# Scaled v of two attention units made together, in a retention and MLP kernel with a rewritten schedule

## The chip, the cores and the metric

The kernel runs on one core of a Trainium2 chip. Its metric is the device time of one execution in microseconds, the median of several runs. The core has five engines with queues of their own: TensorE (PE, with its weight loads shown apart as PEld), VectorE (DVE), ScalarE (ACT), GpSimd (POOL) and SyncE (SP). Here POOL does little but issue the loads from memory that convert float32 to bfloat16; SP issues the transposing copies and the stores.

## The reference

There are 8 batches, 8 heads, 576 positions and 64 numbers per head. First comes causal attention without a softmax, in which a score is multiplied by a power of a per-head number `gamma`; its output, laid out as 4608 tokens of 512 numbers, goes through two matrix products with an exact GELU between them.

```python
scores = (1.0 / np.sqrt(D_)) * np.matmul(q, k.transpose(0, 1, 3, 2))
gamma = 1.0 - 2.0 ** (-5.0 - np.arange(H))
Dmat = np.where(rel >= 0, gamma[:, None, None] ** rel[None], 0.0)   # rel = row - column
x = np.matmul(scores * Dmat, v)          # then as 4608 x 512 tokens
h = x @ w_in                             # 512 -> 2048
out = (0.5 * h * (1.0 + erf(h / sqrt(2)))) @ w_out   # 2048 -> 512
```

## The kernel before

**Attention units.** The attention is done in chunks of 128 positions, with a running state carried from chunk to chunk. A *unit* is one chunk of one batch, all 8 heads (the last chunk has 64 positions; there one unit, a *tail*, holds two batches). Units come in pairs, two batches `j = 0, 1` of the same chunk; there are 36 units, and four units make a block of 512 tokens. For a unit the kernel loads q, k and v (`load_unit`, line 506; the copies on POOL are lines 518 and 522), turns q and k (on PE for units 0 to 9, `turn`, by transposing copies on SP later), multiplies them (`scores`), masks the scores on DVE (`chunk_masked`, `masked`), and multiplies by v (`inner`). The decay by `gamma` is split into a factor on v's rows and one on the output. The first factor is `dv`, one number per row and head; v times `dv` is the tile `vh` (`scaled_v`, line 819), made either by one DVE operation of 128x512 (line 826) or by eight ACT operations of 128x64, one per head (line 829). The list `VH_ACT` says which units take ACT. `vh` is read by `inner` and by `state`, which adds k times v to the running state `u`; a product with the state (`cross`) completes a later chunk. Units 0 to 3, and other units of chunk 0, use v itself in `inner`.

**The MLP.** For each of nine blocks the 512 tokens x 2048 hidden numbers are made in pieces. The weights of the first layer come as eight loads `wi0` to `wi7` (line 528), those of the second as `wo0` to `wo7` (line 531). In blocks 2 to 8 the hidden numbers fall in four parts per block, and a part is done either plainly (four pieces of 4 products with 512 columns) or as a *unit* in Strassen's manner: seven products for eight, each of 4 products with 256 columns, with sums before and after on DVE and ACT. `LAYOUTS` says which: `'10'` is two units interleaved, `'2'` one, `'p3'` a plain part. In block 0 the pieces of the pairs listed in `WIDE` take all 512 tokens in one product; the others follow the units, 128 tokens at a time. The second layer of blocks 1 to 8 is always in Strassen's manner.

**What sets the order.** The program is unrolled in Python, and the order on every engine is written by a planner (`Plan`) when the program is built: every operation has an assumed duration, dependencies and a due time, and the planner takes the next one that can start. The constants at the head (lines 168 to 202) are its knobs: `SHIFT`, `GAP_A`, `GAP_B`, `BEFORE`, `HOLD`, `LOOK` place attention stretches between products, `EASE` holds back `vh`, `ORDER` is the order of the loads on POOL, `SECOND` and `PRODUCTS` that of the Strassen products. Where PE has nothing to do before 16 us of planned time, the planner puts in products on zeros (`warm`); they are instructions like others. Semaphores follow from the dependencies, so a real delay is a wait.

**Buffers.** Loads go into `N_LD = 4` slots, each for a pair's q, k and v. `N_VH = 5` buffers of one unit each hold `vh`, `N_RET = 3` (for either half) the masked scores. The pair `kept`, units 2 and 3, has tiles of its own, since its state is wanted late.

Of the kernel before, what the change touches and what calls it, by code (L numbers as in the profile page):

```python
# [107 lines left out]
def kernel(  # L108
# [9 lines left out]
    nc = tc.nc  # L118
# [42 lines left out]
    def slot_of(i):  # L161
# [24 lines left out]
    GAP_A = 0.0  # L186
    GAP_B = 1.3
    SHIFT = {4: -1.5, 5: -11.5, 6: 1.0, 7: 3.0, 8: 4.0, 9: -1.5, 10: 1.0, 11: 1.0, 12: 1.5, 13: -3.0, 14: -1.0, 15: -0.5, 16: -5.0, 17: -4.5, 18: -1.5, 19: 3.5, 20: 6.5}
# [12 lines left out]
    PRODUCTS = "3251647"  # L201
# [276 lines left out]
    touched = {}  # L478
# [201 lines left out]
    def state(bp, ci):  # L680
# [115 lines left out]
    def gone(nm):  # L796
# [8 lines left out]
        elif kind == "st_b":  # L805
            for i in pair_of[key]:
                vh_ring.give(T["pe"] + 0.3)
                read(i, "state")
# [10 lines left out]
    def scaled_v(i, engine, heads=(0, H)):  # L819
        ci = units[i][1]  # L820
        if "vh" not in st[i]:
            vh_ring.take()
            st[i]["vh"] = vh_pool.tile([128, H, D], BF16, tag="vh", name="vh")
        vh = st[i]["vh"]
        if engine == "dve":
            nc.vector.tensor_tensor(vh, loaded[i][1], dv[:, :, ci:ci + 1].to_broadcast([128, H, D]), op=ALU.mult)  # L826
        else:
            for h in range(*heads):
                nc.scalar.activation(vh[:, h], loaded[i][1][:, h], AF.Copy, scale=dv[:, h, ci:ci + 1])  # L829
        if heads[1] == H:  # L830
            read(i, "v")
# [48 lines left out]
    for i in range(N_U):  # L880
# [14 lines left out]
        if i not in fine and i not in tails:  # L895
# [6 lines left out]
            add(f"inner{i}", "pe", 0.23, [f"mask{m}.1" for m in duo] + [f"land v{i}" if i in raw else f"vh{i}"], lambda i=i: inner(i),  # L902
# [23 lines left out]
        else:  # L926
# [3 lines left out]
            add(f"in_a{n}", "pe", 0.125, [f"mask{n}.0"] + [f"vh{m}" for m in duo], lambda: None, due + 4, DRAIN, banks=2, mode="quad")  # L930
            add(f"in_b{n}", "pe", 0.4, [f"in_a{n}", f"u{bp},{ci},0"] + ([f"u{bp},{ci - 1},1"] if ci else []), lambda: None,
                due + 4, DRAIN, mode="quad")
    for i in v_order:
        due = need[group_of[i]] + 3.0 if i not in kept else need[group_of[pair_of[1, 1][0]]] - 2.0
        n = v_order.index(i)
        room = lambda i=i, due=due: max(0.0 if "vh" in st[i] else vh_ring.at(), due - EASE if group_of[i] > 3 else 0.0)
        before = ["dv", f"land v{i}"] + ([f"vh{v_order[n - 1]}"] if n else [])
        if i in VH_ACT:
            step_ = H // PARTS
            for p in range(PARTS):  # L940
                name = f"vh{i}" if p == PARTS - 1 else f"vh{i}.{p}"
                add(name, "act", 0.2625 * step_, [f"vh{i}.{p - 1}"] if p else before,
                    lambda i=i, p=p, step_=step_: scaled_v(i, "act", (p * step_, p * step_ + step_)), due + p / PARTS, at=None if p else room)
        else:
            add(f"vh{i}", "dve", 0.6, before, lambda i=i: scaled_v(i, "dve"), due if group_of[i] > 1 or i in kept else VH_DUE, at=room)
    order_of_states = [(bp, ci) for bp in range(B // 2) for ci in range(NCI - 1)]
    for bp, ci in order_of_states:
        pair = pair_of[bp, ci]
        deps = [f"vh{i}" for i in pair] + [f"land k{i}" for i in pair if i]
# [714 lines left out]
```

## Time and profile before

| what | value |
|---|---|
| median of 3 runs | 281.17 us (280.98 to 282.06) |
| profiled execution, its own time | 281.36 us |
| its span, first to last instruction | 279.5 us |
| PE, weight loads, DVE, ACT, POOL busy | 271.7, 215.7, 229.8, 176.2, 110.2 us |
| scaled v on ACT | 152 operations, 41.8 us |
| scaled v on DVE | 17 operations, 11.5 us |
| loads of q, k, v and weights on POOL | none after 200 us |

The span is cut at the first and last instruction; the profiled execution's own time has 1.86 us around it. Of a group of instructions the profile gives the count, the engine time that they cover together, and the mean length of one; on engines that overlap neighbours the mean is larger than the time per instruction. In the timeline an instruction's end is less certain than its start, for PE above all, so distances between starts are used here. Some PE records are missing, so that a count in the timeline can be one or two short.

### The profile page before, as it was taken

What the parts mean: (1) busy time and instruction counts of PE and PEld (TensorE: products, weight loads), DVE (VectorE), ACT (ScalarE), POOL (GpSimd) and SP (SyncE); (2) the same over time, 40 slices, a digit from 0 to 9 for tenths busy, and PEclk for the clock granted to TensorE, in tenths of its full rate; (3) what the DMA queues carried; (4) which work ended last, traced back from release to release, by engine and by line L of the source; (5) the groups of instructions that cost most, each with busy time, mean ns of one, the idle gap of its engine ahead of it and who ended that gap; (6) DMA issues with size and microseconds to landing.
All of it is one profiled execution on the core that took longest, in us unless ns stands there. A gap on an engine that the chain in (4) does not pass through costs nothing.

```text
span 279.5 us, 8688 instructions
## 1 busy us (share of the span) xinstructions
PE 271.7 (97%) x3607; PEld 215.7 (77%) x3623; DVE 229.8 (82%) x440; ACT 176.2 (63%) x434; POOL 110.2 (39%) x139
## 2 busy tenths in 40 slices
PE   7899999999999999999999999999999999999995
PEld 2584566578888688858886888778888888888784
DVE  5950757499999997899989999988799989958841
ACT  7586425567839974795189625982695379618741
POOL 8967869847546067710526448305000000000000
PEclk9999999999999999999999999999999999999999
DMA  9999999999999999999999999999700040013013
GB/s 154 165 187 172 191 169 178 136 231 144 131 131 138 214 114 142 145 198 166 130 220 115 118 139 243 145 112 94 196 2 2 6 150 4 2 38 115 0 40 113
DMA packets 152374, 35.55 MB, mean 127 GB/s; under 512 B 141072, under 2 KB 148240, under 8 KB 152336
## 3 DMA queue, kind: packets, MB, share of 16 engines
q0 software_dynamic: 115792, 17.97, 101.3%
q1 hardware_dynamic: 34912, 16.26, 34.3%
q10 hardware_dynamic: 1632, 0.79, 1.1%
q8 instruction: 28, 0.46, 0.7%
q14 instruction: 10, 0.08, 0.1%
HBM read 36.70 MB, written 9.44 MB: 165 GB/s over the span
## 4 chain that ended last, share of the span: by engine, by line
PE 78%; DMA 11%; POOL 7%; issue 1%; ACT 1%; DVE 0%; POOLq 0%; ACTq 0%
PE oT L231 37%; PE zT L231 11%; PE hT L231 8%; PE yT L231 7%; DMA qk_ld<-in_k_dram 5%; PE o_ps L231 4%; DMA qk_ld<-in_q_dram 3%; DMA w_in<-in_moe_w_in_dram 3%; POOL qk_ld L522 3%; PE sc L231 2%; PE u_ps L231 2%; POOL v_ld L522 2%; POOL qk_ld L518 1%; POOL w_in L528 1%; ACT g L1217 0%
## 5 line engine op out<-in xcount | busy, mean ns | idle before, releaser
L231 PEld LDWEIGHTS <-g 128*128 128x128 bf16 x576 | 55.0, 98 | 13.1 <-DVE g L1004 0.3
L231 PEld LDWEIGHTS <-w_in 128*128 128x128 bf16 x528 | 47.2, 98 | 15.8 <-issue 0.2
L231 PEld LDWEIGHTS <-wi_sum 128*128 128x128 bf16 x460 | 44.6, 98 | 7.8 <-issue 0.9
L231 PE MATMUL hT<-xT,w_in 128*128 128x256 bf16 (+2 forms) x334 | 49.7, 292 | 0.6
L1104 ACT ACTIVATE g<-hT 128x512 bf16<-128x512 f32 (+1 forms) x58 | 32.1, 555 | 23.4 <-PE hT L231 22.6
L231 PE MATMUL oT<-w_out,g 128*128 128x256 bf16 (+1 forms) x315 | 45.4, 293 | 0.3 <-issue 0.2
L829 ACT ACTIVATE vh<-v_ld,dv 128x64 bf16<-128x64 bf16 x152 | 41.8, 345 | 1.4 <-DVE qkT L573 1.3
L1248 ACT COPY o_sb<-oT 128x512 f32<-128x512 f32 (+1 forms) x27 | 14.5, 539 | 42.2 <-PE oT L231 35.2
L231 PEld LDWEIGHTS <-s 128*128 128x128 bf16 x384 | 37.1, 98 | 4.7
L522 POOL DMA_DIRECT2D qk_ld<-in_q_dram x31 | 27.7, 896 | 31.5 <-DMA qkT<-qk_ld 23.7
L522 POOL DMA_DIRECT2D v_ld<-in_v_dram x31 | 27.9, 903 | 14.6 <-issue 5.0
L231 PE MATMUL oT<-w_sum,s 128*128 128x256 bf16 x256 | 31.8, 273 | 0.0
L231 PE MATMUL oT<-w_sum,g 128*128 128x256 bf16 x256 | 31.3, 273 | 0.0
L522 POOL DMA_DIRECT2D qk_ld<-in_k_dram x31 | 28.0, 903 | 5.8 <-DMA v_ld<-in_v_dram 5.2
L1217 ACT ACTIVATE g<-zT 128x512 bf16<-128x512 f32 x46 | 26.2, 605 | 2.2 <-PE zT L231 1.5
L657 DVE TENSOR_TENSOR ret<-sc,msk 128x512 bf16<-128x512 f32 x36 | 23.1, 680 | 0.5 <-PE sc L231 0.5
L860 DVE TENSOR_TENSOR xT<-o_ps,dqT 128x512 bf16<-128x512 f32 x26 | 16.7, 680 | 0.6 <-PE o_ps L231 0.6
L826 DVE TENSOR_TENSOR vh<-v_ld,dv 128x512 bf16<-128x512 bf16 x17 | 11.5, 683 | 6.6 <-DMA v_ld<-in_v_dram 6.6
L573 DVE COPY qkT<-qk_ps 128x512 bf16<-128x512 bf16 x17 | 6.7, 420 | 12.3 <-PE qk_ps L235 12.3
L1196 DVE TENSOR_TENSOR q<-q,zT 128x512 f32<-128x512 f32 x23 | 14.9, 681 | 2.1 <-PE zT L231 1.9
L1254 DVE TENSOR_TENSOR o_sb<-o_sb,oT 128x512 f32<-128x512 f32 (+1 forms) x18 | 11.2, 622 | 6.4 <-PE oT L231 4.0
L1226 DVE TENSOR_TENSOR zT<-q,zT 128x512 f32<-128x512 f32 x23 | 15.6, 690 | 1.0 <-PE zT L231 0.6
(174 smaller groups left out, 461.2 us busy)
## 6 DMA issues: line engine op xcount, KB each, us to landing
out_dram<-o_sb SPq DMA_DIRECT2D x29, 256.0 KB, 3.4
qk_ld<-in_k_dram POOLq DMA_DIRECT2D x31, 128.0 KB, 8.0
qk_ld<-in_q_dram POOLq DMA_DIRECT2D x31, 128.0 KB, 8.0
v_ld<-in_v_dram POOLq DMA_DIRECT2D x31, 128.0 KB, 7.6
w_in<-in_moe_w_in_dram POOLq DMA_DIRECT2D x8, 256.0 KB, 8.0
w_out<-in_moe_w_out_dram POOLq DMA_DIRECT2D x8, 256.0 KB, 7.9
out_dram<-o_sb SPq DMA_DIRECT2D x9, 128.0 KB, 2.4
v_ld<-in_v_dram POOLq DMA_DIRECT2D x8, 64.0 KB, 6.3
```

What stands on the lines that cost most here:

```text
L231: return nc.tensor.matmul(*args, **more)
L522: nc.gpsimd.dma_start(dst, src[2 * bp + j, :, ci * C:ci * C + C, :].rearrange("h s d -> s h d"))
L657: nc.vector.tensor_tensor(r, t, by, op=ALU.mult)
L826: nc.vector.tensor_tensor(vh, loaded[i][1], dv[:, :, ci:ci + 1].to_broadcast([128, H, D]), op=ALU.mult)
L829: nc.scalar.activation(vh[:, h], loaded[i][1][:, h], AF.Copy, scale=dv[:, h, ci:ci + 1])
L860: nc.vector.tensor_tensor(dst, o, dqT[:, :, ci * C:ci * C + C], op=ALU.mult)
L1104: nc.scalar.activation(g_of(t, m0)[:, m0 % 2:m0 % 2 + n, m0 // 8, lo:hi], hT, AF.Gelu)
L1196: nc.vector.tensor_tensor(q_, q_, chain[key]["Z"][1], op=ALU.subtract)
L1217: nc.scalar.activation(target(key, what), chain[key][n][1], AF.Gelu)
L1226: nc.vector.tensor_tensor(to, chain[key]["q"], z, op=ALU.add)
L1248: nc.scalar.copy(target(key, what), chain[key][n][1])
L1254: nc.vector.tensor_tensor(to, to, chain[key][n][1], op=ALU.add)
```

## The change

**The scaled v.** `scaled_v` now makes both units of a pair at once. The tile `vh` has room for two units, and there are three such buffers where there were five single ones. On ACT one operation per head covers both units (128 x 2 x 64 in one instruction); on DVE it's still one operation of 128x512 per unit, one behind the other. It starts when the v of both units has landed. A buffer comes free when the state product of the pair has read it. For the kept pair, v of both units now lies in one tile, `v_kept`, that one operation can read. Tails stay as they were, one operation of 128x64 per head.

**The schedule, searched anew.** The knobs have other values: fewer mask buffers (`N_RET` 2 for 3), another list for ACT, seven wide pairs in block 0 instead of five, another order of loads (`pos` first, q, k and v of units 1 to 3 ahead of most weights), other places for the attention stretches, block 12's scores no longer apart, block 4 with one pair interleaved less, block 6 with three Strassen units and a plain part instead of four units, block 8 with its parts in another order, another order of first-layer products within a unit. All instruction orders differ from those before.

```diff
-    N_VH = 5
-    N_RET = 3
+    N_VH = 3
+    N_RET = 2
-    VH_ACT = [6, 8, 10, 11, 12, 13, 14, 15, 16, 17, 19, 21, 22, 24, 27, 28, 31, 34, 35, 37]
+    VH_ACT = [4, 8, 10, 11, 12, 13, 14, 15, 17, 18, 19, 20, 21, 22, 23, 26, 29, 31, 34, 36]
-    SLACK = 0.2
+    SLACK = 0.05
-    WIDE = [2, 6, 14, 10, 4]
+    WIDE = [0, 14, 2, 6, 12, 4, 10]
-    GAP_A = 0.0
-    GAP_B = 1.3
+    GAP_A = 6.3
+    GAP_B = 0
-    APART = [6, 7, 12]
-    BEFORE = 6.1
+    APART = [6, 7]
+    BEFORE = 5.2
-    LOOK = 16
-    HOLD = 5.6
-    LAYOUTS = {2: ['10', '2', 'p3'], 3: ['01', '2', 'p3'], 4: ['1', '02', 'p3'], 5: ['01', '2', 'p3'], 6: ['01', '23'], 7: ['01', '23'], 8: ['10', '3p2']}
-    LEAD = 8.9
-    SPREAD = 7.7
-    EASE = 6.8
-    ORDER = ("k2 wi4 q1 q2 k3 pos k1 wi0 q3 v1 v3 v2 wi3 wi6 wi1 wi7 v4 q4 wi5 k5 wi2 k4 q5 v5 wo0 wo4 wo1 wo5 q9 "
-             "k7 k6 wo6 q6 q8 v10 q7 wo2 v6 wo7 v9 wo3 k10 q10 v7 k8 k9 v8").split()
+    LOOK = 12
+    HOLD = 6
+    LAYOUTS = {2: ['10', '2', 'p3'], 3: ['01', '2', 'p3'], 4: ['01', '2', 'p3'], 5: ['01', '2', 'p3'], 6: ['01', '2', 'p3'], 7: ['01', '23'], 8: ['2', '30', 'p1']}
+    LEAD = 9.0
+    SPREAD = 7.8
+    EASE = 9
+    ORDER = ("pos q1 k1 q3 k3 v2 q2 k2 v1 wi0 v3 wi4 wi7 wi1 wi3 wi2 wi5 wi6 v4 wo4 k5 k4 q5 q4 wo0 v5 q8 wo1 wo5 "
+             "q9 v7 k7 v10 wo2 wo6 q6 wo7 wo3 q7 v6 k6 k10 q10 k8 k9 v9 v8").split()
-    PRODUCTS = "3251647"
+    PRODUCTS = "3251476"
...
-                loaded[i] = (const.tile([128, 2, H, D], BF16, name=f"qk_ld{i}"), const.tile([128, H, D], BF16, name=f"v_ld{i}"))
+                if i == slot_of(i):
+                    v_kept.append(const.tile([128, 2, H, D], BF16, name="v_kept"))
+                else:
+                    tiles_of(slot_of(i))
+                loaded[i] = (const.tile([128, 2, H, D], BF16, name=f"qk_ld{i}"), v_kept[0][:, i - slot_of(i)])
...
+        vh_ring.give(T["pe"] + 0.3)
         for i in pair_of[bp, ci]:
-            vh_ring.give(T["pe"] + 0.3)
             read(i, "state")
...
-    def scaled_v(i, engine, heads=(0, H)):
-        ci = units[i][1]
-        if "vh" not in st[i]:
+    def scaled_v(n, engine, heads=(0, H)):
+
+        ci, duo = units[n][1], pair_with(n)
+        if "vh" not in st[n]:
             vh_ring.take()
-            st[i]["vh"] = vh_pool.tile([128, H, D], BF16, tag="vh", name="vh")
-        vh = st[i]["vh"]
+            t = vh_pool.tile([128, 2, H, D], BF16, tag="vh", name="vh")
+            for i in duo:
+                st[i]["vh"] = t[:, i - n]
+            st[n]["vh both"] = t
+        t = st[n]["vh both"]
+        if n in kept:
+            v_ld = v_kept[0]
+        else:
+            v_ld = slots[n][1]
         if engine == "dve":
-            nc.vector.tensor_tensor(vh, loaded[i][1], dv[:, :, ci:ci + 1].to_broadcast([128, H, D]), op=ALU.mult)
+            for i in duo:
+                nc.vector.tensor_tensor(t[:, i - n], v_ld[:, i - n], dv[:, :, ci:ci + 1].to_broadcast([128, H, D]), op=ALU.mult)
         else:
             for h in range(*heads):
-                nc.scalar.activation(vh[:, h], loaded[i][1][:, h], AF.Copy, scale=dv[:, h, ci:ci + 1])
+                nc.scalar.activation(t[:, :len(duo), h], v_ld[:, :len(duo), h], AF.Copy, scale=dv[:, h, ci:ci + 1])
...
+    v_order = [n for n in v_order if n == slot_of(n)]
     for i in v_order:
-        n = v_order.index(i)
+        n, many = v_order.index(i), len(pair_with(i))
-        before = ["dv", f"land v{i}"] + ([f"vh{v_order[n - 1]}"] if n else [])
+        before = ["dv"] + [f"land v{m}" for m in pair_with(i)] + ([f"vh{v_order[n - 1]}"] if n else [])
         if i in VH_ACT:
-                add(name, "act", 0.2625 * step_, [f"vh{i}.{p - 1}"] if p else before,
+                add(name, "act", (0.2625 if many == 1 else 0.315) * step_, [f"vh{i}.{p - 1}"] if p else before,
         else:
-            add(f"vh{i}", "dve", 0.6, before, lambda i=i: scaled_v(i, "dve"), due if group_of[i] > 1 or i in kept else VH_DUE, at=room)
+            add(f"vh{i}", "dve", 0.6 * many, before, lambda i=i: scaled_v(i, "dve"), due if group_of[i] > 1 or i in kept else VH_DUE, at=room)
```

The dictionary `SHIFT` has other values too (left out above), and the places that named `vh` of each unit as a dependency now name the pair's.

More of the change, by code (lines that the diff above doesn't have):

```diff
@@ L901 @@
                     lambda i=i, e=e: chunk_masked(i, e), due + 2.0 + 0.01 * e, at=ret_ring.at if not e else None)
-            add(f"inner{i}", "pe", 0.23, [f"mask{m}.1" for m in duo] + [f"land v{i}" if i in raw else f"vh{i}"], lambda i=i: inner(i),
+            add(f"inner{i}", "pe", 0.23, [f"mask{m}.1" for m in duo] + [f"land v{i}" if i in raw else f"vh{slot_of(i)}"], lambda i=i: inner(i),
                 due + 4, DRAIN, banks=1, mode="col")
@@ L929 @@
             add(f"mask{n}.0", "dve", 0.6, last + ["msk", f"mask{n}.1"], lambda n=n: masked(n, 0), due + 2.01)
[L930 removed]
+            add(f"in_a{n}", "pe", 0.125, [f"mask{n}.0", f"vh{n}"], lambda: None, due + 4, DRAIN, banks=2, mode="quad")
             add(f"in_b{n}", "pe", 0.4, [f"in_a{n}", f"u{bp},{ci},0"] + ([f"u{bp},{ci - 1},1"] if ci else []), lambda: None,
                 due + 4, DRAIN, mode="quad")
+    v_order = [n for n in v_order if n == slot_of(n)]
     for i in v_order:
         due = need[group_of[i]] + 3.0 if i not in kept else need[group_of[pair_of[1, 1][0]]] - 2.0
[L935 removed]
+        n, many = v_order.index(i), len(pair_with(i))
         room = lambda i=i, due=due: max(0.0 if "vh" in st[i] else vh_ring.at(), due - EASE if group_of[i] > 3 else 0.0)
[L937 removed]
+        before = ["dv"] + [f"land v{m}" for m in pair_with(i)] + ([f"vh{v_order[n - 1]}"] if n else [])
         if i in VH_ACT:
@@ L948 @@
         pair = pair_of[bp, ci]
-        deps = [f"vh{i}" for i in pair] + [f"land k{i}" for i in pair if i]
+        deps = [f"vh{pair[0]}"] + [f"land k{i}" for i in pair if i]
         if ci:
```

9 lines of the change are left out of this document (5 added, 4 removed).

## The prediction

> **What bounds the kernel now.** I began with the page. The tensor engine (PE) is busy 97% of the span, at the full granted clock in every slice.
>
> ```profile
> PE 271.7 (97%) x3607; PEld 215.7 (77%) x3623; DVE 229.8 (82%) x440; ACT 176.2 (63%) x434; POOL 110.2 (39%) x139
> PEclk9999999999999999999999999999999999999999
> ```
>
> A busy PE need not be a full PE, so next come the waits of PE alone (what it waited for: us in total, times, longest).
>
> ```profile
> PE warm L231 <- DVE ln_scale L352: 1.2, 1, 1.2
> PE qk_ps L235 <- DMA qk_ld<-in_q_dram: 0.9, 2, 0.6
> PE qk_ps L235 <- DMA qk_ld<-in_k_dram: 0.6, 2, 0.4
> PE zT L231 <- ACT g L1217: 0.4, 1, 0.4
> PE oT L231 <- issue: 0.2, 1, 0.2
> ```
>
> Behind the first 1.2 us, the start of the kernel, PE waits 2.1 us in all. ScalarE (ACT), whose work the change cuts, holds PE once, for 0.4 us. Third, the timeline of PE: start, length, tile, number of instructions, and in brackets the wait before it.
>
> ```profile
> 13.35 0.62 PE L231 MATMUL hT<-xT,w_in 128*128 128x128 bf16 x8
> ...
> 17.54 0.41 PE L231 MATMUL o_ps<-ret,v_ld 128*64 128x128 bf16 x8
> 17.89 11.54 PE L231 MATMUL hT<-xT,w_in 128*128 128x128 bf16 x99
> 29.26 1.07 PE L235 MATMUL qk_ps<-ident,qk_ld 128*128 128x128 bf16 x16
> ...
> 41.97 0.62 PE L235 MATMUL qk_ps<-ident,qk_ld 128*128 128x128 bf16 x8 [0.35 <-DMA qk_ld<-in_q_dram]
> ...
> 53.66 0.61 PE L235 MATMUL qk_ps<-ident,qk_ld 128*128 128x128 bf16 x8 [0.39 <-DMA qk_ld<-in_k_dram]
> 54.10 1.03 PE L231 MATMUL oT<-w_out,g 128*128 128x512 bf16 x4
> 55.06 0.64 PE L231 MATMUL o_ps<-ret,vh 128*64 128x128 bf16 x16
> ...
> 57.55 1.04 PE L231 MATMUL hT<-xT,w_in 128*128 128x256 bf16 x8
> 58.42 1.03 PE L231 MATMUL oT<-w_out,g 128*128 128x512 bf16 x4
> 59.28 0.93 PE L231 MATMUL hT<-xT,w_in 128*128 128x256 bf16 x7
> ```
>
> The prices are in the distances between starts. Eight products of 256 columns take 58.42 - 57.55 = 0.87 us, 0.109 each. Four of 512 take 59.28 - 58.42 = 0.86, 0.215 each. From 17.89 to 29.26 run 64 products of 128 columns and 36 of 512 (the program's count; a record is missing): 11.37 - 36 x 0.215 = 3.63, so 0.057 each. A step from plain products to an attention stretch costs 55.06 - 54.10 - 0.86 = 0.10 us. From 17.9 to 276.3 us the kernel is a queue of products on PE with hardly a hole. So I count what PE executes, then what it waits for.
>
> Before 17.9 us it's otherwise. There the loads come one by one on POOL's queue, and PE fills its waits with products on zeros (`warm`). The POOL timeline and the chain of waits tell how a weight lands:
>
> ```profile
> 8.35 2.67 POOL L522 DMA_DIRECT2D v_ld<-in_v_dram x3
> 10.94 3.05 POOL L528 DMA_DIRECT2D w_in<-in_moe_w_in_dram x4
> ```
>
> ```profile
> 10.94 8.08 DMA w_in<-in_moe_w_in_dram
> ```
>
> A q, k or v piece takes POOL 0.87 us, a weight 0.76. The early pieces land 5.9 to 6.5 us after their issue (q, k and v loads of the first 11 us); the weight issued at 10.94 took 8.08.
>
> **The change part by part.** The counts are from the two programs' instruction orders.
>
> *Fewer ScalarE scalings.* 152 of them become 80 double ones and 24 single (the tails).
>
> ```profile
> L829 ACT ACTIVATE vh<-v_ld,dv 128x64 bf16<-128x64 bf16 x152 | 41.8, 345 | 1.4 <-DVE qkT L573 1.3
> L405 ACT ACTIVATE near<-far,ln_scale 128x128 f32<-128x128 f32 x8 | 2.4, 386 | 0.0
> ```
>
> One costs 41.8/152 = 0.275 us of the engine. A double one isn't in the trace: at least 0.275, at most the 0.386 of a whole 128x128 operation. I take the 0.305 of one in the row of eight (2.4/8), which has the same 128 elements. ACT then spends 80 x 0.305 + 24 x 0.275 = 31.0 us for 41.8, 10.8 less (4.3 to 13.2). Seven copies of turned q and k move from DVE (0.42 each) to ACT (0.585), 4.1 us back. On the path this is worth at most the 0.4 us wait above, and I take 0. On the other side a pair waits for the later of its two v loads and its two-head step grows from 0.55 to 0.61 us, with GELUs and bank copies queued behind it on ACT. No PE wait in the trace is for a scaled v (those that wait on it are the state's copies and POOL), so that cost is 0 now; if ten ACT pairs each came 0.3 us late, it would be 3 us. Three pair buffers hold six units where five did: no loss of room, 0. Two mask buffers in place of three: DVE's mask could wait for the previous inner product, which the order puts ahead of the next scores on PE; 0, covered by the products in between. v of the kept units in one tile: 0.
>
> *The products.* Block 6 loses one of its four Strassen-like units, 23 become 22: 28 products of 256 columns go, 28 x 0.109 = 3.05, and 16 of 512 come, 16 x 0.215 = 3.44. Seven wide pairs instead of five in block 0: 64 products of 128 columns go (3.65), 16 of 512 come (3.44). Together **+0.2 us** on PE. DVE loses a unit's chain of 0.69 us steps (about 3 us) and four scalings (2.7); it was behind no PE wait but is 82% busy, so 0.
>
> *The switches.* PE goes from plain products into attention 27 times, not 30: 3 x 0.10 = **-0.3 us**.
>
> *The start.* PE gets 7 more warm products of 512 columns, 23 for 16: 7 x 0.215 = 1.5 us. They are instructions and run whether needed or not. Before, 40 products of the first layer are done when the last inner product of units 0 to 3 ends (17.54 + 0.35 = 17.89); after, 8 are. So the same warm work with no more waits puts the stream 1.5 us later: the floor. The other end is the load order. Now q, k, v of units 1 to 3 come ahead of most weights and `pos` ahead of all: the second weight (wi4), that the first product needs, is the eleventh load. POOL: 1.34 + 0.2 (`pos`) + 8 x 0.87 + 0.76 + 0.87 = 10.1 us, landing after 6.4 (as the third early v) to 8.1 (as the weight at 10.94): 16.5 to 18.2. DVE is tight too: v1 lands near 13.9 and both scalings of pair 0 (2 x 0.68) stand on DVE ahead of unit 2's masks (2 x 0.68 and a 0.41 of decay), so unit 2's inner product comes near 17.0, then 1.1 us of warm, and the first product near 18.2. Behind it 0.45 + 0.35 to the end of the last inner product: 17.3 to 19.0, with 8 x 0.057 = 0.5 of first-layer work done, against 17.89 with 2.3 done. The loss is (17.3 - 0.5) to (19.0 - 0.5), less 15.6: 1.2 to 2.9. I take **+2.0**, nearer the floor, as the latest DVE end is reached only if v1 is as late as I put it.
>
> *The stretch to 54 us.* Here PE waited for q and k loads (0.35, 0.39) and once for issue (0.16). With PE 2 us behind and the same bytes in the queue, those end before PE asks: -0.9 (to 0 if the new order brings them later). A new wait comes at block 0's end: the scores of units 4 and 5 stand right behind their last turn, where four wide products stood before. Turn start to copy start is 0.42 (29.26 to DVE's copy at 29.68), the copy 0.42 to 0.585; less the 0.45 of the turns themselves: 0.4 to 0.6. I take +0.6. Sum **-0.3**. Two stores of block 0 now stand ahead of SP's first transposes; these are due for the tail unit's scores near 60 us, some 9 us later (before: issued 51.5, that stretch from 61.1): 0.
>
> *Sum.* 0.2 - 0.3 + 2.0 - 0.3 = +1.6 us. The profiled execution took 281.36 us (span 279.5 and 1.86 around it), 0.19 over the median of 281.17. So 281.36 + 1.6 = 282.96, less 0.19: **282.8 us**.
>
> **Two rules weighed.** The row first: 0.86 us for four products of 512 columns. The Trainium skill ("TensorE: Matmul & The Clock Gate", Back-to-back issue gap) gives about 131 ns each in a real kernel and about 216 ns alone. By 131 the 32 more wide products would cost 4.2 and not 6.9 us, and the sum would be 280.1; the trace shows 0.215, so I stay. The Trainium skill ("Perfetto Trace Analysis", Identifying the Most-Contended Engine) says that matmul busy time does not tell the headroom of PE and the weight loads' share does: 77% here. By that PE has slack and the relief of ACT may show, rival 3 below. The spacing of 0.109 and the 2.1 us of waits speak against it.
>
> **The rivals.**
> 1. *The loads pay the start back.* The queue feeds PE until 53.7 us; if the new order brings q and k so that PE never waits there, and the start stays at its floor, the sum is 0.2 - 0.3 + 1.5 - 1.5 (all q and k waits, the two before 12 us too) = -0.1, and with the 0.4 and 0.2 waits -0.7: 280.5 to 281.1, a little faster. It decides in this favour if PE's plain stream begins by 17.3 us and no new wait of 0.3 us stands before 54. For it: the waits are there. Against it: warm products cannot be given back.
> 2. *The scaled pairs come late.* Ten ACT pairs at 0.3 us: 282.8 + 3 = 285.8; half of them, 284.3. For it: one v now holds two units and the steps are longer. Against it: ACT idles 37% of the span.
> 3. *Relief of ACT and DVE shows on PE.* All waits gone, and 0.8 us that three attention stretches take beyond their like (0.2 to 0.3 each): 281.17 + 0.2 - 0.3 + 1.5 - 2.9 = 279.7. For it: DVE is full in places (20.0 of 20 us from 60 to 80). Against it: so few waits name either.
> 4. *The double operation saves nothing* (0.55 each): ACT stays at 41.8 + 8.8 us, still far from full; the time is my forecast's.
>
> **How the numbers follow.** Forecast 0.47 (281.9 to 283.9), with rival 4 in it; rival 1 0.27; rival 2 0.17; rival 3 0.09. A measurement of this kernel tells about 0.5%, 1.4 us: 279.8 to 282.6 is the same. The forecast is two thirds above 282.6, rival 2 wholly: slower 0.32 + 0.17 = 0.49. Faster: half of rival 3 and a sixth of rival 1, 0.09. Same: 0.42. The range leaves a tenth on each side: 280.3 (under rival 1) to 285.0 (inside rival 2).
>
> **What would show it.** Right: PE's long first-layer stretch starts its stream with 8 products done at 18 us or later; no PE wait for q or k at 42 and 54 us, one of about half a us before the scores near 33; PE waits after 60 us still about 1 us; vh on ACT near 31 us. Wrong: PE waits on ACT or o_ps/u_ps stretches that start late (rival 2), or the second block's second layer starting no later than 68.2 us (rival 1).

## The result, and the profile after

The changed kernel takes 283.12 us (median of 8 runs, 282.14 to 284.32); the kernel before, in runs on the same chips, 281.41 us (280.98 to 282.06). The ratio is 1.0057 with a 95% interval of 1.0034 to 1.0080: slower, by 1.7 us, and 0.3 us over the forecast of 282.8. The profiled execution is one of the slower ones: 283.69 us, span 281.7. A second set of runs of the same kernel (below, `e9_again`) gave 282.88 us, with a profiled execution of 282.60; behind 34 us the two profiles differ in one wait of PE, which matters for the reading.

The page of the changed kernel: busy time by engine, the granted clock in 40 slices, and the group of the scaled v on ACT.

```profile
PE 275.2 (98%) x3570; PEld 214.0 (76%) x3570; DVE 220.1 (78%) x422; ACT 171.9 (61%) x390; POOL 110.3 (39%) x139
PEclk9999999999999999999999999999999999999999
L842 ACT ACTIVATE vh<-v_ld,dv 128x128 bf16<-128x128 bf16 (+1 forms) x104 | 32.6, 387 | 0.0
```

DVE's busy time fell by 9.7 us and ACT's by 4.3 us, yet the span grew by 2.2 us and PE's busy time by 3.5 (about 2.0 of that because 16 records of PE are missing in the profile before: the same products, all recorded, take 273.7 in the run with two mask buffers below). Scaled v on ACT went from 41.8 to 32.6 us. What PE waited for (us in total, times, longest) in the same execution:

```profile
PE warm L231 <- DVE ln_scale L352: 1.2, 1, 1.2
PE yT L231 <- issue: 1.2, 1, 1.2
PE sc L231 <- DVE qkT L577: 0.3, 1, 0.3
PE qk_ps L235 <- DMA qk_ld<-in_q_dram: 0.2, 1, 0.2
```

The waits for q and k at 42 and 54 us and the one for a GELU are gone. A wait before scores is new (0.3 us of it marked), and so is one of 1.2 us that names no tile and no engine. Their places, in the timeline of PE (start, length, tile, count, wait before it):

```profile
16.76 1.31 PE L231 MATMUL warm<-u_sb 128*128 128x512 bf16 x6
17.91 0.61 PE L231 MATMUL hT<-xT,w_in 128*128 128x128 bf16 x8
18.45 0.41 PE L231 MATMUL o_ps<-ret,v_kept 128*64 128x128 bf16 x8
...
33.58 0.75 PE L231 MATMUL sc<-qkT 64*64 64x128 bf16 x32 [0.29 <-DVE qkT L577]
...
53.26 0.61 PE L235 MATMUL qk_ps<-ident,qk_ld 128*128 128x128 bf16 x8
...
69.14 1.04 PE L231 MATMUL oT<-w_out,g 128*128 128x256 bf16 x8
...
85.99 0.27 PE L231 MATMUL yT<-xT,wi_sum 128*128 128x256 bf16 x1
87.42 0.93 PE L231 MATMUL yT<-xT,wi_sum 128*128 128x256 bf16 x7 [1.15 <-issue]
```

Three marks in this timeline cut each execution into comparable pieces: the end of the last early inner product (here 18.79), the first product of block 1's second layer (69.14; up to it both programs execute the same work apart from warm products and 0.2 us of wide pairs), and the end of PE's last product. All are us from the start of the span; the "work start" is the first mark less 0.057 us for each small first-layer product done before it (8 after, 32 before).

| kernel | work start | second layer of block 1 | last product ends | start to second layer | second layer to end |
|---|---|---|---|---|---|
| before | 16.06 | 68.02 | 276.31 | 51.96 | 208.30 |
| changed | 18.34 | 69.14 | 278.49 | 50.80 | 209.35 |
| changed, again | 18.25 | 69.17 | 277.33 | 50.92 | 208.16 |
| six warm products fewer | 16.95 | 69.13 | 277.23 | 52.18 | 208.10 |
| changed, loads of before | 16.49 | 67.95 | 277.21 | 51.46 | 209.26 |
| changed, single scalings | 18.02 | 69.18 | 281.55 | 51.17 | 212.37 |
| before, loads of the change | 17.32 | 68.81 | 278.91 | 51.50 | 210.09 |
| before, two mask buffers | 16.16 | 67.82 | 276.17 | 51.66 | 208.35 |
| before, planned anew | 16.12 | 67.58 | 280.26 | 51.46 | 212.69 |

So the change loses 2.2 to 2.3 us at the start, gets 1.0 to 1.2 back by the second layer of block 1, and from there to the end it's 0.1 us shorter than before in one execution and 1.05 longer in the other, which had the wait at 86 us. Single differences in this table are worth little under 0.4 us: three executions with before's order up to the second mark (before, two mask buffers, planned anew) reach it at 68.02, 67.82 and 67.58 us.

### The profile page after: what moved, and what is told of

It reads as the page before. It is cut to its first block, busy times and chain, and to the rows that moved or that the text cites. A ratio compares the mean times of both kernels' runs of the same rounds, so it can differ in the third digit from the quotient of the medians.

```text
span 281.7 us, 8529 instructions
## 1 busy us (share of the span) xinstructions
PE 275.2 (98%) x3570; PEld 214.0 (76%) x3570; DVE 220.1 (78%) x422; ACT 171.9 (61%) x390; POOL 110.3 (39%) x139
## 4 chain that ended last, share of the span: by engine, by line
PE 92%; DMA 2%; ACT 2%; issue 1%; DVE 1%; POOL 0%; POOLq 0%; DVEq 0%; ACTq 0%
PE oT L231 40%; PE hT L231 17%; PE zT L231 9%; PE yT L231 6%; PE o_ps L231 5%; PE sc L231 3%; DMA qk_ld<-in_q_dram 2%; PE qk_ps L235 2%; PE u_ps L231 2%; ACT g L1232 2%; PE warm L231 2%; PE xT__5072 L231 0%; PE xT__3951 L231 0%; PE xT__3487 L231 0%; PE xT__3418 L231 0%
## 5 line engine op out<-in xcount | busy, mean ns | idle before, releaser
L231 PEld LDWEIGHTS <-w_in 128*128 128x128 bf16 x488 | 46.0, 98 | 19.6
L231 PE MATMUL hT<-xT,w_in 128*128 128x512 bf16 (+2 forms) x312 | 52.4, 319 | 0.0
L231 PEld LDWEIGHTS <-wi_sum 128*128 128x128 bf16 x440 | 42.7, 98 | 7.7 <-issue 1.3
L526 POOL DMA_DIRECT2D qk_ld<-in_q_dram x31 | 27.9, 899 | 38.0 <-DMA qkT<-qk_ld 21.7
L1119 ACT ACTIVATE g<-hT 128x512 bf16<-128x512 f32 (+1 forms) x58 | 33.8, 589 | 14.5 <-PE hT L231 14.1
L842 ACT ACTIVATE vh<-v_ld,dv 128x128 bf16<-128x128 bf16 (+1 forms) x104 | 32.6, 387 | 0.0
L526 POOL DMA_DIRECT2D v_ld<-in_v_dram x29 | 26.2, 902 | 6.4 <-DMA qk_ld<-in_q_dram 4.6
L1232 ACT ACTIVATE g<-zT 128x512 bf16<-128x512 f32 x44 | 25.5, 606 | 1.4 <-DVE zT L1241 1.3
L522 POOL DMA_DIRECT2D qk_ld<-in_q_dram x8 | 5.5, 689 | 35.5 <-PE u_ps L231 34.1
L577 DVE COPY qkT<-qk_ps 128x512 bf16<-128x512 bf16 x10 | 4.0, 421 | 17.7 <-PE qk_ps L235 17.7
L848 ACT CAST u_sb<-u_ps 128x512 bf16<-128x512 f32 x15 | 8.8, 588 | 11.0 <-PE u_ps L231 10.5
```

The lines of the kernel that those rows point to most:

```text
L231: return nc.tensor.matmul(*args, **more)
L526: nc.gpsimd.dma_start(dst, src[2 * bp + j, :, ci * C:ci * C + C, :].rearrange("h s d -> s h d"))
L842: nc.scalar.activation(t[:, :len(duo), h], v_ld[:, :len(duo), h], AF.Copy, scale=dv[:, h, ci:ci + 1])
L848: ins = (nc.vector.tensor_copy if engine == "dve" else nc.scalar.copy)(u_sb[t if bp >= FINE else ci % 2], u_bank[1])
L1119: nc.scalar.activation(g_of(t, m0)[:, m0 % 2:m0 % 2 + n, m0 // 8, lo:hi], hT, AF.Gelu)
L1232: nc.scalar.activation(target(key, what), chain[key][n][1], AF.Gelu)
```

## The experiments

### The double operation, undone

In the changed kernel each ACT operation over both units becomes two, one per unit; the order on every engine stays.

```diff
-                nc.scalar.activation(t[:, :len(duo), h], v_ld[:, :len(duo), h], AF.Copy, scale=dv[:, h, ci:ci + 1])
+                for u in range(len(duo)):
+                    nc.scalar.activation(t[:, u, h], v_ld[:, u, h], AF.Copy, scale=dv[:, h, ci:ci + 1])
```

> The changed kernel with its double ScalarE operations split in two again (one per unit and head, 184 in all for 104), everything else in the same order. Theory (ScalarE is off PE's path): vh on ACT goes from 32.6 us to 184 x 0.275 = 50.6 us, the time stays at 283.1 within 0.6. Rival (the double operation is what holds the time where it is, or its relief shows on PE): slower by more than 1 us, 284.2 or above.

Measured: 285.71 us (285.32 to 286.75), ratio to before 1.0156 [1.0135, 1.0177]: 2.6 us over the changed kernel. Scaled v on ACT took 47.7 us for 32.6. The waits of PE in this kernel:

```profile
PE yT L231 <- issue: 1.4, 1, 1.4
PE warm L231 <- DVE ln_scale L352: 1.2, 1, 1.2
PE zT L231 <- ACT g L1233: 0.7, 3, 0.3
PE oT L231 <- ACT q L1251: 0.5, 2, 0.3
PE oT L231 <- DVE ret L661: 0.4, 1, 0.4
```

ACT and DVE hold PE six times; in the list of the changed kernel neither does behind 34 us. One place, ACT's timeline of this kernel and what PE did there:

```profile
72.12 1.07 ACT L843 ACTIVATE vh<-v_ld,dv 128x64 bf16<-128x64 bf16 x4
73.09 0.36 ACT L1251 COPY q<-oT 128x256 f32<-128x256 f32 x1
```

```profile
73.49 1.03 PE L231 MATMUL oT<-w_out,g 128*128 128x256 bf16 x8 [0.18 <-ACT q L1251]
```

A bank copy stands behind four single scalings; the order had placed it behind two double ones (0.71 us there). So ACT's relief isn't worth 0 in this order: taken back, it costs 2.6 us. In the two profiles that have the wait at 86 us the loss behind block 1's second layer is 3.0 us: the six waits, of 0.2 to 0.4 us each, are 1.6 of it, and the wait at 86 us is 0.25 longer; the rest is marked as no wait.

### The same, with the order planned for it

As above, and the planner is told the length of two single operations.

```diff
-                add(name, "act", (0.2625 if many == 1 else 0.315) * step_, [f"vh{i}.{p - 1}"] if p else before,
+                add(name, "act", 0.2625 * many * step_, [f"vh{i}.{p - 1}"] if p else before,
```

> The changed kernel with each double scaling of ScalarE as two single ones, as in the run before (285.71 us), but with the planner told their length (0.525 us for a pair's head in place of 0.315), so that the order on each engine is planned for them. Theory A: ScalarE's relief carries time by itself, whatever the order; the 13 us that come back on ScalarE go on delaying GELUs and bank copies: 285.0 to 286.2. Theory B: the 2.6 us were the price of an order planned for shorter operations; planned for the real ones the waits for ScalarE (0.7 + 0.5 us and the 0.3 to 0.5 us in eight places) go away and the time is that of the changed kernel, 282.3 to 283.7.

Measured: 286.43 us (285.96 to 286.58), ratio 1.0180 [1.0164, 1.0195]. Theory B falls: planning for the true length didn't bring the time back. It doesn't prove theory A, since a new order by itself can cost as much (below, "Planned anew").

### The warm products, and what paces the start

The last six warm products of the changed kernel (from 16.76 us) are left out; the planner still counts their time, so that nothing else moves.

```diff
-                warm(gap)
+                (skipped if T["pe"] > 14.2 else warm)(gap)
```

> The changed kernel without the last six products on zeros (five of 512 columns, one of 128, 1.13 us) that stand ahead of the first first-layer product. Theory (they are a part of the late start): the first hT begins near 16.95 us, when its weight has landed, in place of 17.91; up to 0.6 us of that is waited away again at the turn of units 8 and 9, whose k lands at 52.9; time 282.2 to 282.7. Rival (PE had to wait there anyway): hT still begins after 17.7 and the time stays 283.1. On the issue wait of 1.15 us at product 987: if it belongs to the place in the instruction stream (every 127.8 products from the 92nd), it moves with the six products and splits the yT group after its seventh and not its first product; if it belongs to the work, it stays ahead of the second.

Measured: 282.42 us (282.25 to 283.09), ratio 1.0037 [1.0023, 1.0052], 0.7 under the changed kernel. The table tells that the gain isn't the start's. Work starts 1.4 us earlier (16.95), and the second layer of block 1 begins at 69.13, as with the six products. The chain of waits of this kernel around 50 us (start, length, what):

```profile
38.94 7.04 DMA w_out<-in_moe_w_out_dram
45.98 0.28 issue
46.27 0.87 POOL qk_ld L526
47.14 5.98 DMA qk_ld<-in_k_dram
53.12 0.14 issue
53.25 0.61 PE qk_ps L235 x8
```

The last k that PE turns lands at 53.1 us, no earlier than with the warm products; PE waits 0.81 us for it here, and in the changed kernel, where it landed at 52.9 and 53.2 in the two profiles, PE comes to this turn at 53.26 and 53.29 with no wait at all. What the run gained lies elsewhere: its profile doesn't have the wait at 86 us, and from the second layer to the end it takes 208.10 us, as the second profile of the changed kernel, without that wait too, takes 208.16. The five times also lie within those of the changed kernel (282.14 to 284.32), so that a gain of 0.7 us is itself not certain.

### The order of the loads, both ways

The changed kernel with three settings of before (`ORDER`, `WIDE`, `SLACK`), and the kernel before with those three of the change.

```diff
-    SLACK = 0.05
+    SLACK = 0.2
-    WIDE = [0, 14, 2, 6, 12, 4, 10]
+    WIDE = [2, 6, 14, 10, 4]
-    ORDER = ("pos q1 k1 q3 k3 v2 q2 k2 v1 wi0 v3 wi4 wi7 wi1 wi3 wi2 wi5 wi6 v4 wo4 k5 k4 q5 q4 wo0 v5 q8 wo1 wo5 "
-             "q9 v7 k7 v10 wo2 wo6 q6 wo7 wo3 q7 v6 k6 k10 q10 k8 k9 v9 v8").split()
+    ORDER = ("k2 wi4 q1 q2 k3 pos k1 wi0 q3 v1 v3 v2 wi3 wi6 wi1 wi7 v4 q4 wi5 k5 wi2 k4 q5 v5 wo0 wo4 wo1 wo5 q9 "
+             "k7 k6 wo6 q6 q8 v10 q7 wo2 v6 wo7 v9 wo3 k10 q10 v7 k8 k9 v8").split()
```

> The changed kernel with three knobs of before: the order of the loads, the five wide pairs and the slack of the first 20 us. Theory (the start is the cost): 16 warm products of 512 columns again, PE content 1.4 us less by its counts, the free first-layer stream from 17.9 us with 32 products done ahead of it, and the waits for q and k near 42 and 54 us come back; time 281.6 to 282.5, some 1.0 us below the changed kernel. Rival (the cost is the scaled pairs or the later schedule): 283.1 within 0.5.

> The kernel before (single scalings, five buffers) with three settings of the changed one: the order of the loads, the seven wide pairs of block 0 and the slack. It takes the start and the stretch to 54 us by themselves. By the prediction's terms: the start 2.0 us later (6 more warm products are 1.3 of it), the waits for q and k of 0.9 us gone, wide pairs -0.2: 282.2 to 283.2 us. Rival, the loads pay the start back: no wait for q or k before 54 us and the start at its floor, 281.0 to 281.8 us.

Measured: 282.67 us (282.23 to 282.92), ratio 1.0041 [1.0027, 1.0056], for the change with the old loads, a little above the expectation; 284.44 us (283.39 to 285.45), ratio 1.0109 [1.0073, 1.0144], for before with the new loads, above both. The whole time mixes two things, and the table parts them. Up to the second layer of block 1, the old settings bring the changed kernel from 69.14 to 67.95, before's own 68.02, and the new ones bring before from 68.02 to 68.81. So the new order of loads, with the wide pairs and the slack that go with it, costs 0.8 to 1.2 us there, whichever scaling is used; the three settings were not tried one by one. Behind that mark both hybrids lose 1.1 and 1.8 us against the kernel whose settings they otherwise have: the planner wrote them another order that nobody searched.

### The third mask buffer

The kernel before with two mask buffers; every engine has the same instructions in the same order.

```diff
-    N_RET = 3
+    N_RET = 2
```

> The kernel before with two mask buffers in place of three (N_RET 2) and nothing else; every engine has its instructions in the order of before, so only the room of the mask differs. The prediction costed the third buffer at 0, covered by the scores that stand between two inner products. By that: 281.2 to 281.8 us, ratio 0.999 to 1.002, and the waits of PE as before. Rival: of the 2.0 us that pairs with before's other settings cost, the missing third buffer carries most, as DVE's mask of a unit then waits for the inner products of the unit two back: 282.4 to 283.4 us, with waits of PE on ret or of DVE's mask on o_ps that before does not have.

Measured: 281.32 us (281.02 to 281.93), ratio 0.9995 [0.9973, 1.0017]. The prediction's 0 for the buffer holds.

### Pairs in the settings of before

The changed program with all of before's settings, except three pair buffers and two mask buffers; the cut shows it against the kernel before, without the rest of the code for pairs.

```diff
-    N_VH = 5
-    N_RET = 3
+    N_VH = 3
+    N_RET = 2
...
-                nc.scalar.activation(vh[:, h], loaded[i][1][:, h], AF.Copy, scale=dv[:, h, ci:ci + 1])
+                nc.scalar.activation(t[:, :len(duo), h], v_ld[:, :len(duo), h], AF.Copy, scale=dv[:, h, ci:ci + 1])
```

> The new scaled v alone: the changed program with all knobs of before except the three pair buffers and two mask buffers. Theory (the double operation is worth nothing on the path and costs nothing): 281.4 within 0.6, vh on ACT about 72 x 0.31 + 24 x 0.275 = 29 us. Rival 2 (pairs come late): 282.5 or more, with PE waits for o_ps or u_ps. Rival 3 (relief shows): 280.6 or less.

Measured: 283.37 us (282.93 to 284.75), ratio 1.0075 [1.0055, 1.0095], 2.0 us over before. It isn't the mask buffer. It looks like the price of pairs, and the next run says why it can't be read so.

### Planned anew

The kernel before with one figure of the planner nearer to the trace: the instructions are the same but for one copy that changes engine, in another order behind the first 884 products.

```diff
-                add(name, "act", 0.2625 * step_, [f"vh{i}.{p - 1}"] if p else before,
+                add(name, "act", 0.275 * step_, [f"vh{i}.{p - 1}"] if p else before,
```

> The kernel before with one figure of its planner changed: a single scaled head of v is planned with 0.275 us, as the trace has it, in place of 0.2625. The instructions are the same but for one bank copy that goes to the other engine; loads and the first 884 products stand as before, behind them 497 of PE's places and some 190 each of ScalarE's and DVE's hold another instruction. It asks whether the 2.0 us of pairs in before's settings are the pairs' own. Theory A: they are the pairs' (later or longer scalings), and another order of the same instructions costs nothing: 281.0 to 281.9 us. Theory B: before's settings (due times, gaps, shifts) fit before's order, and an order that was not searched loses about as much as the pairs did: 282.4 to 283.5 us, in waits of 0.2 to 0.5 us behind 75 us.

Measured: 285.82 us (285.34 to 287.02), ratio 1.0162 [1.0138, 1.0186]: 4.4 us over before, more than theory B had it, and not in small waits but in one. DVE's timeline of this kernel, and PE's:

```profile
208.03 0.69 DVE L1004 TENSOR_TENSOR g<-g 128x1024 bf16<-128x1024 bf16 x1
208.63 0.68 DVE L1004 TENSOR_TENSOR s<-g,s 128x1024 bf16<-128x1024 bf16 x1
209.23 0.69 DVE L826 TENSOR_TENSOR vh<-v_ld,dv 128x512 bf16<-128x512 bf16 x1
209.83 0.68 DVE L860 TENSOR_TENSOR xT<-o_ps,dqT 128x512 bf16<-128x512 f32 x1
210.43 0.69 DVE L1200 TENSOR_TENSOR xT__4292<-xT__4292,q 128x512 f32<-128x512 f32 x1
211.03 0.69 DVE L1200 TENSOR_TENSOR xT__4300<-xT__4300,q 128x512 f32<-128x512 f32 x1
211.63 0.68 DVE L1209 TENSOR_TENSOR q<-xT__4292,t 128x512 f32<-128x512 f32 x1
```

```profile
208.58 1.04 PE L231 MATMUL zT<-xs,wi_sum 128*128 128x256 bf16 x8
212.37 1.01 PE L231 MATMUL xT__4292<-xs,wi_sum 128*128 128x256 bf16 x4 [2.75 <-DVE q L1209]
213.17 1.06 PE L231 MATMUL xT__4300<-xs,wi_sum 128*128 128x256 bf16 x4
214.03 1.60 PE L231 MATMUL oT<-w_out,g 128*128 128x256 bf16 x8
215.46 1.04 PE L231 MATMUL oT<-w_sum,s 128*128 128x256 bf16 x8
```

The Strassen chain that frees PE's bank (`more`, line 1200, and `dif`, line 1209) stands behind other work of 0.6 us each on a DVE that is full. PE waits 2.75 us. What comes next is in the windows (from:to, length, busy time and count of PE, PEld, DVE, ACT, POOL, granted clock, DMA):

```profile
209.60:212.40 2.80, 0.05 (x2) 0.03 (x1) 2.80 (x6) 0.41 (x1) 0.00 (x0) 0.88 0.00 0
212.40:214.00 1.60, 1.60 (x8) 1.10 (x8) 1.60 (x3) 0.59 (x1) 0.00 (x0) 0.50 0.00 0
214.00:215.40 1.40, 1.40 (x10) 1.02 (x8) 1.40 (x4) 1.14 (x4) 0.00 (x0) 0.58 0.00 0
215.40:216.50 1.10, 1.10 (x13) 0.99 (x11) 1.00 (x2) 0.44 (x1) 0.00 (x0) 1.00 0.00 0
```

The clock falls to half while PE still waits (0.88 on average in the window of the hole) and stands there for 2.8 us of products: the 16 products from 212.37 to 215.46 take 3.09 us, where 16 x 0.109 are 1.74. Of the 4.4 us that this kernel loses behind the second layer of block 1, 2.75 are the wait and 1.35 the slow clock behind it. All five executions have a mean granted clock of 0.994, where those of before have 0.998 to 1.000, which fits a stretch of 3.4 us at half clock in each of them. So an order of the same instructions that was not searched can cost more than all terms of the prediction together, and the 2.0 us of the pairs, the 3.3 of the single scalings planned anew and the later losses of the two hybrids can't be told from that. What pairs alone are worth in before's order stays open.

### The wait at 86 us

The changed kernel again, as it is; and with 24 more warm instructions at its start (8 products of 512 columns as 32 of 128), the rest in the same order.

```diff
-        product(t, lhsT=zeros[:, :128], rhs=zeros, start=True, stop=True)
+        made[0] += 1
+        for c in range(0, 512, 128):
+            nc.tensor.matmul(t[:, c:c + 128], lhsT=zeros[:, :128], rhs=zeros[:, c:c + 128], start=True, stop=True)
```

> The changed kernel once more, unchanged but for the order of two conditions in one line, on the chip and in the rounds of the other three. Its eight times so far go from 282.1 to 284.3 us. If the wait behind the 987th product belongs to the order and is in each execution, the profile has it whatever the time of this execution. If it comes and goes, the profile has it at a time over 283.0 and has none or a shorter one at a time under 282.5. The median: 282.4 to 283.6.

> The changed kernel with its first 8 warm products of 512 columns as 32 of 128 (24 instructions more, about 0.1 us of PE, the rest in the same order). It asks what the 1.2 us wait marked issue at 86 us is, which both profiled executions of this order had behind the 987th product. If it hangs on the number of the instruction (PE's program comes in pieces from memory, one for about 128 products), it moves 24 products forward, into the second-layer stretch oT<-w_out,s that starts near 82.6 us, behind its 9th product (within 4), and none is left behind the first yT near 86. If it hangs on the place (what that yT or the operations around it need), it stays where it was. If it hangs on the run, there is none in either. The time: 282.2 to 284.4 us.

Measured: 282.88 us (282.60 to 283.28), ratio 1.0061 [1.0044, 1.0078], for the kernel again, and 282.71 us (282.53 to 283.00), ratio 1.0051 [1.0036, 1.0066], with the 24 more. Neither profile has the wait. The same place of the changed kernel, in its second profile (282.60 us):

```profile
86.02 1.05 PE L231 MATMUL yT<-xT,wi_sum 128*128 128x256 bf16 x8
```

So it comes and goes with the execution, as the expectation had it: there in a profile of 283.69 us, not in one of 282.60 (a little over the 282.5 named there). It was also there, 1.40 us long, in the kernel with single scalings, behind the same product, the 987th. The shifted kernel was to tell the number of the product from the place in the work, and didn't, since it doesn't wait anywhere near. What speaks for a late piece of program is the line of the page on the queue that brings instructions, and the times of its transfers:

```profile
q8 instruction: 28, 0.46, 0.7%
```

Those 28 transfers for 3570 products are one per 127.5; the planner itself counts a new piece every 127.8 products from the 92nd, which puts the end of its eighth at 92 + 7 x 127.8 = 987. The transfer before that end began at 83.86 us in the profile with the wait (5.7 us behind the start of the product that ends the piece before; what held it is not settled), at 84.58 with single scalings (wait of 1.40), and at 83.30 in the second profile of the changed kernel (none). PE went on 3.6 and 3.9 us behind the start of the transfer.

The other kernels tell more. Apart from these two, three waits of over 0.2 us marked issue stand in the fourteen profiles behind the start. These are two of them, from the changed kernel with the loads of before and from the pairs in the settings of before:

```profile
63.70 4.42 PE L231 MATMUL hT<-xT,w_in 128*128 128x256 bf16 x39 [0.34 <-issue]
186.54 0.22 PE L231 MATMUL sc<-qkT 64*64 64x64 bf16 x2 [0.29 <-issue]
```

The first is behind the 732nd product, and by the same count a piece ends at 92 + 5 x 127.8 = 731; the second is behind the 2393rd, and a piece ends at 92 + 18 x 127.8 = 2392. The third (0.52 us at 133.90, in the kernel before with the loads of the change) is within some ten products of the end at 1626; records are missing there. The work is another each time, and the number is one at which a piece ends: the wait goes with the number. When it comes stays open. In these places PE went on 2.4 to 3.9 us behind the start of the transfer, but elsewhere it passed an end 2.5 us (two mask buffers, the 2520th product) and 2.8 us behind it (the second profile of the changed kernel, the 987th) without a wait. So it's well supported that PE stands there for its program, though no run moved the wait on purpose. The Trainium skill ("Runtime: NRT & Kernel Launch", Instruction fetch mechanics) says that the sequencer fetches its program in blocks of 16 KiB while it executes, and that the cost of crossing a block is "mostly hidden". The size agrees (0.46 MB in 28 transfers are 16.4 KB each); that it's hidden holds for the other places of this kernel, and not for the 987th product in one of its two profiles.

### A version that might beat both

Six warm products fewer, with v of unit 10 as the last load, so that the late k lands earlier; and the same with block 6 of four Strassen units again.

```diff
-             "q9 v7 k7 v10 wo2 wo6 q6 wo7 wo3 q7 v6 k6 k10 q10 k8 k9 v9 v8").split()
+             "q9 v7 k7 wo2 wo6 q6 wo7 wo3 q7 v6 k6 k10 q10 k8 k9 v9 v8 v10").split()
```

```diff
-    LAYOUTS = {2: ['10', '2', 'p3'], 3: ['01', '2', 'p3'], 4: ['01', '2', 'p3'], 5: ['01', '2', 'p3'], 6: ['01', '2', 'p3'], 7: ['01', '23'], 8: ['2', '30', 'p1']}
+    LAYOUTS = {2: ['10', '2', 'p3'], 3: ['01', '2', 'p3'], 4: ['01', '2', 'p3'], 5: ['01', '2', 'p3'], 6: ['01', '23'], 7: ['01', '23'], 8: ['2', '30', 'p1']}
```

> The changed kernel without the last six warm products (282.42 us before) and with v of unit 10 as the last load, 11 places later than in the change, so that the k and q behind it land about 0.87 us earlier. The run before waited 1.3 us for k of which 0.9 should go: 281.3 to 281.9 us, a wait for k of at most 0.4 us. Rival: the order behind 54 us, which the planner makes anew, gives it back: 282.3 to 283.2 us.

> The run beside it (v of unit 10 last, six warm products fewer) with block 6 of four units again, as the kernel before has it: 28 products of 256 columns for 16 of 512, by the counts -0.39 us of PE and one unit's chain more on DVE. If that block has room on DVE: 0.2 to 0.5 us less than the run beside it, 280.9 to 281.7 us. If the change left the fourth unit out for DVE's sake, 0 to 1 us more than it, with waits of PE on xs or xT between 190 and 225 us.

Measured: 283.35 us (282.57 to 283.63), ratio 1.0062 [1.0039, 1.0086], and 284.01 us (283.13 to 284.77), ratio 1.0089 [1.0061, 1.0118]. In the first the wait for k is gone, but the planner wrote a new order behind it, in which the scores wait 0.8 us for a transposing copy and second-layer products 0.6 us for ACT. Its profiled execution, the slowest of the four, also starts its work 0.9 us later than the kernel with six warm products fewer (17.8 for 16.95): a turn of four products takes 0.61 us until 11 us, where that kernel's takes 0.40 from 10 us on. In the second, behind the second layer of block 1, PE takes 208.63 us for 208.03: the fourth unit executes 0.39 us less and loses 1.0, of which 0.63 are one wait for a GELU at 210.66 us. None beats the kernel before.

## Why the prediction was right, and where not

The time (282.8 for 283.1), the sign and the leading reason (the new order of loads costs more at the start than it gives back) were right. The sum of the steps came out within 0.3 us, and that is in part luck: the stretch to block 1's second layer gained 0.5 us more than forecast, and the median holds a wait that was not foreseen, of 1.2 us in some executions. By the marks of the table, against the second profile of the changed kernel, which lacks the wait at 86 us:

| part | forecast | measured |
|---|---|---|
| start, to the last early inner product | +2.0 | +2.2 |
| from there to block 1's second layer (the stretch, wide pairs) | -0.5 | -1.0 |
| from there to the end (block 6's unit, switches, relief of ACT) | +0.1 | -0.1 |
| around the span | 0 | +0.2 |
| wait at 86 us, in some executions | 0 | +1.2 or 0 |

- **The start.** The step counted 40 first-layer products done before 17.89 us in the kernel before; it's 32 (four groups of 8). With 32 the same working gives a loss of 0.7 to 2.4, not 1.2 to 2.9; the measured 2.2 lies in both. The stream began at 18.79 with 8 products done, as forecast (18 us or later, 8 done).
- **The floor that wasn't one.** That the warm products "run whether needed or not" was true, and "the stream 1.5 us later: the floor" was not: without six of them work starts 1.4 us earlier and arrives at 69.13, as with them. What fixes that point is the last turned k, landing near 53 us, and 15.9 us of products that the order has behind the turn (69.14 - 53.26); before it was 14.4 behind a turn at 53.66 (68.02 - 53.66). The loss of 1.1 us at 69 us belongs to the loads and to where the order has the turn, and not to the warm products. The two loads experiments show that part of it at 0.8 to 1.2.
- **The stretch to 54 us.** The waits for q and k went (-0.9) and the wait before the scores came: 0.29 marked and 0.46 from turn to scores beyond the turns' own 0.45, for the forecast 0.4 to 0.6. With the wide pairs it was priced at -0.5 and was -1.0 to -1.2; the missing 0.5 is about what executions of one order differ by, and stays unexplained. Start and stretch are two ends of one thing: whatever PE loses early, it doesn't wait for later at the loads.
- **The relief of ACT at 0.** The price of a double operation was right: eight take 2.44 us, 0.305 each, as taken from the row of the decay; the total was 32.6 for 31.0, because most double ones run in groups of two, which take 0.69 (all 80 take 26.3 us, 0.329 each; the 24 single ones of the tails take 6.3, a little less than thought). The step failed in its reasoning, that ACT idles 37% and that the relief is therefore worth at most the 0.4 us wait for it. In the new order its absence costs 2.6 us. The reading is that the old order had room for the single operations and the new one has it not, so that a change of order and of length go together; no run shows that apart, since single operations planned for took 286.43 us. The difference between the two searched orders is near 0 (-0.1 with 0.39 more product time, so about 0.5 gained in waits and switches). That is what the sum was right about, and it's what little there is of rival 3.
- **Two mask buffers at 0, three pair buffers at 0.** The first is shown (281.32 us). Of the second only this: in the changed kernel no PE wait is for a scaled v, so rival 2, pairs that come late, didn't happen.
- **The products.** Seven wide pairs and block 6's unit were priced from the spacings 0.215, 0.109 and 0.057, and these still hold. The fourth unit, cheaper by 0.39 in products, cost 0.6 us more when put back, in an order that the planner made for it. (Block 4's layout only regroups its units; the block with one interleaving less is block 8.) The rule of 131 ns (the Trainium skill, "TensorE: Matmul & The Clock Gate", Back-to-back issue gap), rejected there, shows nowhere in these runs: behind the turn at 53.25, in the kernel without the six warm products, four products of 512 columns take 0.86 us.
- **What was not foreseen.** The wait at 86 us, which stood in no row of before. The sign "PE waits after 60 us still about 1 us" came true with it and by chance. Its size, 1.2 us in part of the executions, is about half of what separates the runs of the changed kernel (282.1 to 284.3) from each other, but only two of its executions were profiled.

Rival 1 is excluded by the second layer's start at 69.14 (its mark was 68.2 at the latest).

## What to carry to other kernels

When an order written for one set of lengths keeps an engine full, neither "this engine idles a third of the time" nor the waits listed in the old profile price a change of that engine's work: undo the one part inside the new order and measure. Removing filler at the start only pays if the next thing that PE waits for also comes earlier, so look for the last load that PE needs, and for how much work the order has left behind it. And before putting a loss down to an edit, plan the unchanged instructions anew: here that alone moved the time by 4.4 us.

## What the runs showed of the hardware

- **After one hole of 2.75 us the clock was halved.** It fell before the hole was over; behind it the granted clock was 0.50 for 1.6 us and 0.58 for another 1.4, and the first eight products of 256 columns took 0.21 us each for 0.109. The wait of 1.15 us in the changed kernel left it at 1.00 in the stretch behind. The Trainium skill ("TensorE: Matmul & The Clock Gate", HAM oscillation — how this bites in real kernels) states the limit as no gap of PE over some 3.4 us; a shorter one was enough here.

```profile
86.20:87.40 1.20, 0.07 (x1) 0.00 (x0) 1.02 (x2) 0.20 (x1) 0.35 (x1) 1.00 1.67 143
87.40:90.00 2.60, 2.58 (x24) 2.31 (x24) 1.62 (x3) 1.98 (x5) 2.60 (x4) 1.00 1.44 251
```

  These two windows are the changed kernel's, in the columns named above; the clock is the third number from the right.
- **PE very likely stands for its own program now and then.** It stood 0.29 to 1.40 us, with nothing that it waits for, at five places in five executions, and each is at or close to a product at which a piece of its instructions ends (the 732nd, the 987th twice, near the 1626th, the 2393rd).
- **Twice the elements in a ScalarE operation cost little.** 128 x 2 x 64 took 0.305 us of the engine in rows of eight (2.44) and 0.329 over all 80 (26.3), 128 x 64 took 0.275 (41.8 for 152) and 0.259 (47.7 for 184).
